# Attention and a feed-forward on one core: which tiles TensorE turns, a replanned order, and one pair's scores in float32

## The chip, the cores and the metric

The kernel runs on one core of a Trainium2 chip. The metric is the device time of one execution in microseconds (us); several executions are timed and their median is compared. PE is TensorE, PEld its weight loads, DVE VectorE, ACT ScalarE, POOL GpSimd, SP SyncE, whose queue (SPq) issues the DMAs here.

## The reference: what is computed

Two stages follow each other. The first is attention with a capped score over 4 batches, 12 heads, 448 tokens and 64 channels per head; the second is a feed-forward over all 4 x 448 = 1792 tokens.

```python
scores = scale * np.matmul(q, k.transpose(0, 1, 3, 2))
scores = cap * np.tanh(scores / cap)
attn = np.exp(scores - max); attn = attn / (sum + 1e-09)
x = np.matmul(attn, v)                       # [1792, 768] after the heads are joined
h = x @ w_in                                 # [1792, 1024]
solu = h * softmax(h)
ln = (solu - mean) / np.sqrt(var + 1e-06) * g_ln
out = ln @ w_out                             # [1792, 768]
```

(The middle lines are abridged.) Everything is float32, so a product of two float32 matrices is either one float32 matmul, which the trace shows as two instructions, or three matmuls of the float32r type: each operand is split into a high part and a low rest, and high x high, high x low and low x high are added.

## The kernel before

**Attention.** Two heads make a pair, six pairs a batch, 24 pairs in all. `front(u)` loads the pair's keys and queries (tile raw, line 362), splits them into hi and lo (lines 371 and 372), and computes the scores in three chunks of 128 keys by three float32r products (tile s, line 382) and the remaining 64 keys by one float32 product (line 387). ACT takes tanh out of PSUM (lines 392 and 410) into ea and eb and then exp in place (line 395). `back(u)` multiplies the exponentials by the values in float32 (tile pv, lines 463 and 468), and sums them over the keys by small matmuls into tile z (line 477). From pair 8 on DVE adds chunks first (lines 442 to 448), which halves that work. `divide(b)` turns a batch's sums into reciprocals (lines 527 to 536) and multiplies xt, the transposed attention output, by them.

**Feed-forward.** The 1792 tokens are 14 tiles of 128; tiles 0 to 2 need batch 0 alone, 3 to 6 also batch 1, 7 to 9 batch 2, 10 to 13 batch 3. `ff_in(t)` splits the tile into xh and xl (lines 558 and 559) and runs 36 matmuls of 512 columns (lines 568 to 570) into the two PSUM buffers of the ring m, then `keep`, exp, the sums and the normalisation on DVE, ACT and POOL (lines 575 to 615). `ff_out(t)` runs 48 matmuls of 384 columns (lines 678 to 680), through the same ring m. Between them the normalised tile has to be turned, so that its channels lie on partitions. There are two ways, and one condition chooses, at lines 617 and 640:

```python
if BY_DVE <= t < NTILE - BY_PE:
```

If it holds, DVE transposes 32 x 32 blocks (line 620), SP issues 16 DMAs that gather the blocks (line 625), a copy makes the high part (line 649) and DVE the low part (line 650). If not, PE turns the tile by eight transposes against an identity, four into each of two PSUM buffers (line 664), a copy out of PSUM makes the high part (line 667), and DVE the low part (line 668). The buffers come from m, or from the scores' ring s for tiles 9 and later. Before the change BY_DVE is 1 and BY_PE 1, so tiles 1 to 12 go by DVE and the DMAs, and tiles 0 and 13 by PE.

**Weights.** w_in and w_out arrive as 64-bit words; ACT and DVE convert each of 12 and 16 chunks (lines 721 to 732) while the first pairs run.

**The order.** Nothing is scheduled by hand. Every piece of work is a `step` with an engine, a cost, a due time and its reads and writes; `Plan.run` simulates the engines, always lets the engine that can start first take the ready step with the earliest due time, and then writes each engine's instructions in that order. Engines execute strictly in that order, so an instruction that has to wait holds everything behind it on its engine. The due times come from the constants at the head of the file (UNIT, AHEAD1, WI_FROM, ...), and the waits between engines from LATENCY, TO_PE and FROM_PE. Copies that ACT or DVE can do go to the one that the planner thinks will end first.

Of the kernel before, what the change touches and what calls it, by code (L numbers as in the profile page):

```python
# [9 lines left out]
F32 = mybir.dt.float32  # L10
# [1 line left out]
I32 = mybir.dt.int32  # L12
CAP_MAX = 40.0
HOLD = 0.1
LATENCY = 0.15
T0 = 4.0
UNIT0 = 0.71
UNIT = 6.29
TILE = 13.13
CUTS0 = (128, 256, 384)  # L20
CUTS1 = (64, 192, 320)
CUTS2 = (128, 256, 384)
CUTS3 = (64, 192, 320)
LATER = 17.82
EARLY = -9.62
LEAD0 = 0.16
LEAD1 = 0.41
LEAD2 = 5.35
LEAD3 = 1.36
AHEAD1 = 21.64  # L30
AHEAD2 = 57.26
AHEAD3 = 79.39
WI_FROM = -0.47
WI_STEP = 2.15
WO_FROM = 1.45
WO_STEP = 4.91
ADDS_FROM = 8
CH1 = -1.8
CH2 = -39.84
REST_AT = -1.96  # L40
EXPA = 0.63
EXPB = -0.6
SUMA = 0.62
SUMB = 4.88
VAL = 4.2
VALSTEP = 0.45
ZAT = 2.64
RAWS = 2
LOS = 1
VS = 2  # L50
WARM = 5
BY_PE = 1
BY_DVE = 1
TURN_AHEAD = 6.88
GATHER = 5.4
HS = 2
# [4 lines left out]
MM448 = 0.2035  # L61
MM384 = 0.1743
TURN = 0.128
SWITCH = 0.1
STAY = 41.15
BIAS = 0.21
TO_PE = 0.25
FROM_PE = 0.2
HEAD1 = 0.11
AF = mybir.ActivationFunctionType  # L70
ALU = mybir.AluOpType
# [72 lines left out]
def PRODUCTS(hi, lo):  # L144

    return (hi, hi), (hi, lo), (lo, hi)
# [34 lines left out]
class Plan:  # L181
# [6 lines left out]
    COPY = "ACT or DVE"  # L188

    def __init__(self, nc, free):  # L190
        self.steps, self.free, self.tiling = [], dict(free), None
        self.copy = {"ACT": nc.scalar.copy, "DVE": nc.vector.tensor_copy}

    def step(self, eng, us, due, emit, reads=(), writes=(), lag=0.0, uses=(), tiling="128x128"):

        n = dict(eng=eng, us=us, tiling=tiling, due=due, emit=emit, lag=lag, deps=[], starts=[], todo=0, outs=[], start=None, i=len(self.steps))
        for t in reads:
            n["deps"] += t.writers
        for t in writes:
            if t.first is None:  # L200
                t.first = n
                if t.prev is not None:
                    n["deps"] += t.prev.writers + t.prev.readers
# [16 lines left out]
    def run(self):  # L220
        for n in self.steps:
            n["todo"] = len(n["deps"]) + len(n["starts"])
            for d in n["deps"] + n["starts"]:
                d["outs"].append(n)
        ready = {eng: [] for eng in ("PE", "ACT", "DVE", "POOL", "SP", self.COPY)}
        for n in self.steps:
            n["at"] = 0.0
            if not n["todo"]:
                ready[n["eng"]].append(n)
        order = []  # L230
        while any(ready.values()):
            best = None
            for eng, free in self.free.items():
                other = {"ACT": "DVE", "DVE": "ACT"}.get(eng)
                ns = ready[eng]
                if other:
                    ns = ns + [n for n in ready[self.COPY] if self.end(n, eng) <= self.end(n, other)]
                if not ns:
                    continue
                first = max(free, min(n["at"] for n in ns))  # L240
                n = min((n for n in ns if n["at"] <= first), key=lambda n: (n["due"], n["i"]))
                us = n["us"] if n["eng"] == eng else n["us"][eng]
                n = min((n for n in ns if n["at"] <= first + self.HOLD * us), key=lambda n: (n["due"], n["i"]))
# [12 lines left out]
            if eng == "PE" and n["tiling"] != self.tiling:  # L256
                n["us"] += SWITCH
                self.tiling = n["tiling"]
            n["start"] = start
            self.free[n["eng"]] = start + n["us"]  # L260
            order.append(n)
            for m in n["outs"]:
                m["todo"] -= 1
                wait = self.WAIT.get((n["eng"], m["eng"]), LATENCY) + n["us"] + n["lag"]
                m["at"] = max(m["at"], start + (wait if any(d is n for d in m["deps"]) else 0.0))
                if not m["todo"]:
                    ready[m["eng"]].append(m)
# [12 lines left out]


def dve(n, rate=1, extra=0):
    return n / rate / 960 + 0.068 + 0.061 * extra
# [3 lines left out]
def body(ctx: ExitStack, tc, kq, v, w_in, w_out, g_ln, out, r_tanh, r_exp, mhalf, sel, sels, ident, gT, xtail, both, guard, general, const=None, loaded=None):  # L287

    nc = tc.nc
    B, NP, P, S = kq.shape  # L290
    D, S = P // 2, S // 2
    NC = S // P
    REST = S - NC * P
# [18 lines left out]
    hi_r, lo_r = ring("hi", 2, [P, 2 * S - REST], F32R), ring("lo", LOS, [P, 2 * S - REST], F32R)  # L312
# [19 lines left out]
    step = plan.step  # L332
# [15 lines left out]
    def front(u):  # L348
# [12 lines left out]
        p.place = [half[j if u % 2 == 0 else 1 - j] for j in range(2)]  # L361
        step("SP", 1.6, due - (1.5 * d if u else 20.0), lambda: nc.sync.dma_start(out=raw.get(), in_=kq[b, p.hp]), writes=[raw], lag=2.0)

        hi, lo = hi_r.new(), lo_r.new()
        at = due - 0.5 * d
        n = 2 * S - REST

        for x in ((slice(0, n),) if u else (slice(0, n - S), slice(n - S, n))):
            part = Buf()
            m, r = x.stop - x.start, slice(REST + x.start, REST + x.stop)  # L370
            step(plan.COPY, copied(m), at, lambda copy, x=x, r=r: copy(out=hi.get()[:, x], in_=raw.get()[:, r]), [raw], [hi, part])  # L371
            step("DVE", dve(m), at, lambda x=x, r=r: nc.vector.tensor_sub(lo.get()[:, x], raw.get()[:, r], hi.get()[:, x].bitcast(F32)), [raw, part], [lo])

        ea, eb = p.ea, p.eb = ea_r.new(), eb_r.new()
        p.chunk = lambda c: ea.get()[:, 2 * c:2 * c + 2] if c < 2 else eb.get()[:, :2]
        p.rest = lambda j: eb.get()[p.place[j], 2]

        def scores(c, pt):
            parts = [(x.get(), y.get()) for x, y in PRODUCTS(hi, lo)]
            for i, (x, y) in enumerate(parts):  # L380
                for j in range(2):
                    nc.tensor.matmul(pt.get()[:, j, :S], lhsT=x[half[j], c * P:(c + 1) * P], rhs=y[half[j], NC * P:], start=(i == 0), stop=(i == len(parts) - 1))  # L382
# [5 lines left out]

        def chunk(c, at):
            pt = s_r.new()  # L390
            step("PE", len(PRODUCTS(0, 0)) * MM448, at, lambda: scores(c, pt), [hi, lo], [pt], tiling="64x128")
            step("ACT", act(2 * S, 0.05), at, lambda: nc.scalar.activation(out=p.chunk(c), in_=pt.get()[:, :, :S], func=AF.Tanh, scale=r_tanh), [pt], [ea if c < 2 else eb])  # L392

        def exp(e, k, at):
            step("ACT", act(k * S), at, lambda: nc.scalar.activation(out=e.get(), in_=e.get(), func=AF.Exp, scale=r_exp), [e], [e])  # L395
# [1 line left out]
        def rest(at):  # L397
            pt = s_r.new()

            def both_rests():  # L400
                scores_rest(pt)
                if old:
                    old.values_rest()

            if old:
                step("PE", 4 * MM448, at, both_rests, [raw, old.v, old.eb], [pt, old.pp], tiling="64x64")["starts"] += old.pp.writers[:-1]
                old.finish()
            else:
                step("PE", 4 * MM448, at, both_rests, [raw], [pt], tiling="64x64")
            step("ACT", act(S, 0.05), at, lambda: nc.scalar.activation(out=eb.get()[:, 2], in_=pt.get()[:, 0, :S], func=AF.Tanh, scale=r_tanh), [pt], [eb])  # L410

        def load_v():
            step("SP", 0.8, due - (d if u else 19.0), lambda: nc.sync.dma_start(out=p.v.get(), in_=v[b, p.hp]), writes=[p.v], lag=2.0)
# [336 lines left out]
    if not general:  # L750

        idle = pv_r.new()

        def warm():
            x = xtail.rearrange("p k d -> p (k d)")
            for i in range(WARM):
                nc.tensor.matmul(idle.get()[:, :2 * P], lhsT=x[:, :P], rhs=x[:, P:], start=True, stop=True)

        step("PE", 0.7 * WARM, -100.0, warm, writes=[idle])
    front(0)  # L760
    for b in range(B):
        for hp in range(NP):
# [56 lines left out]
```

## Time and profile before

| | |
|---|---|
| median of the runs, lowest, highest | 431.03, 430.65, 434.64 us |
| the profiled execution | 435.72 us |
| its span, from first to last instruction | 433.9 us |
| busy, share of the span | PE 95%, PEld 65%, DVE 70%, ACT 55%, POOL 11% |
| mean granted TensorE clock over the span | 0.986 |
| chain that ended last, by engine | PE 56%, DVE 13%, ACT 8%, SPq 8%, DMA 8% |

The chain follows the work back from the last instruction, at each step to what released it. A busy PE is not PE at its peak: matmuls are pipelined, their ends are modelled, and one matmul's record overlaps the next one's. What a piece of PE work costs is therefore read from the start of one group of instructions to the start of the next.

### The profile page before, as it was taken

The page shows a single profiled execution, that of the slowest core. Times are in us where ns is not written, and L with a number is a line of the kernel's source. Part 1 is how long each engine was busy: PE and PEld are TensorE (multiplying, and loading weights), DVE is VectorE, ACT ScalarE, POOL GpSimd, SP SyncE. Part 2 cuts the span into 40 slices and gives each one's busy share as a digit, 9 for nine tenths or more (in the row PEclk, how much of TensorE's full clock was granted, in tenths as well). Part 3 has the DMA queues.
Part 4 walks back from the last instruction along what each step waited for, and adds up shares of the span by engine and source line. Part 5 has one row for each costly group of instructions (what it writes and reads, how often), then busy time and mean ns, then how long its engine had stood idle before and what let it go on. Part 6 is the DMA issues. An engine that isn't in the chain of part 4 may idle for free.

```text
span 433.9 us, 6550 instructions
## 1 busy us (share of the span) xinstructions
PE 410.5 (95%) x2314; PEld 282.3 (65%) x2314; DVE 302.7 (70%) x736; ACT 239.3 (55%) x317; POOL 46.6 (11%) x122
## 2 busy tenths in 40 slices
PE   7789799999997999999999989999999999999894
PEld 4333334667742348888964445666877898998894
DVE  3889979999986899665538499977543984643310
ACT  4889799478776984261339988195321320221220
POOL 2000000022400000112212000011110111211100
PEclk9699899999999999999999999999999999999999
DMA  7778965000234330121223432102011111111111
GB/s 249 282 246 295 315 212 180 2 0 6 59 107 156 128 104 24 44 61 37 71 69 120 130 113 84 63 23 64 23 50 37 51 51 41 63 48 50 57 59 42
DMA packets 25418, 41.43 MB, mean 95 GB/s; under 512 B 5920, under 2 KB 18720, under 8 KB 25376
## 3 DMA queue, kind: packets, MB, share of 16 engines
q1 hardware_dynamic: 25376, 40.92, 29.1%
q8 instruction: 20, 0.33, 0.3%
q14 instruction: 22, 0.18, 0.1%
HBM read 29.10 MB, written 5.51 MB: 80 GB/s over the span
## 4 chain that ended last, share of the span: by engine, by line
PE 56%; DVE 13%; ACT 8%; SPq 8%; DMA 8%; issue 3%; POOL 2%; DVEq 0%; ACTq 0%; POOLq 0%
PE pv L463 8%; PE s L382 7%; SPq L625 7%; PE m L678 7%; PE m L680 6%; PE m L679 6%; PE m L568 6%; PE m L569 6%; PE m L570 5%; DMA wi<-in_w_in 3%; PE s L387 3%; DMA raw<-in_kq 2%; ACT ea L392 2%; PE z L477 2%; DVE rs L535 2%
## 5 line engine op out<-in xcount | busy, mean ns | idle before, releaser
L678 PE MATMUL m<-wo,ln 128*128 128x384 f32 x208 | 71.0, 342 | 0.3 <-DVE h L575 0.3
L679 PE MATMUL m<-wo,ln 128*128 128x384 f32 x208 | 69.8, 336 | 0.4 <-DVE wo L732 0.4
L680 PE MATMUL m<-wo,ln 128*128 128x384 f32 x208 | 69.7, 335 | 0.0
L568 PE MATMUL m<-wi,xh 128*128 128x512 f32 x168 | 66.6, 397 | 0.5 <-DVE ln L668 0.5
L570 PE MATMUL m<-wi,xl 128*128 128x512 f32 x168 | 65.9, 392 | 0.1
L569 PE MATMUL m<-wi,xh 128*128 128x512 f32 x168 | 65.8, 392 | 0.0
L463 PE MATMUL pv<-ea,v 128*64 128x448 f32 x192 | 46.0, 589 | 8.4 <-ACT eb L410 3.3
L392 ACT ACTIVATE ea<-s 128x896 f32<-128x896 f32 x48 | 41.5, 918 | 15.7 <-PE s L382 15.7
L586 ACT ACTIVATE ef<-h,st 128x1024 f32<-128x1024 f32 x14 | 16.1, 1153 | 56.7 <-DVE h L575 33.9
L678 PEld LDWEIGHTS m<-wo,ln 128*128 128x128 f32 x208 | 39.0, 188 | 3.7 <-issue 2.6
L395 ACT ACTIVATE ea<-ea 128x1792 f32<-128x1792 f32 x24 | 40.9, 1702 | 0.5
L679 PEld LDWEIGHTS m<-wo,ln 128*128 128x128 f32 x208 | 39.1, 188 | 2.0 <-DVE wo L732 0.8
L568 PEld LDWEIGHTS m<-wi,xh 128*128 128x128 f32 x168 | 31.5, 188 | 11.6 <-issue 3.8
L680 PEld LDWEIGHTS m<-wo,ln 128*128 128x128 f32 x208 | 39.0, 188 | 0.0
L382 PEld LDWEIGHTS s<-hi 64*128 64x128 f32 x144 | 13.8, 188 | 35.4 <-issue 14.9
L591 POOL TENSOR_SCALAR st<-st 128x1 f32<-128x1 f32 x14 | 8.6, 616 | 260.8 <-ACT ef L586 260.7
L570 PEld LDWEIGHTS m<-wi,xl 128*128 128x128 f32 x168 | 31.5, 188 | 7.3 <-DVE xl L559 0.5
L569 PEld LDWEIGHTS m<-wi,xh 128*128 128x128 f32 x168 | 31.5, 188 | 5.7
L382 PE MATMUL s<-hi 64*128 64x448 f32 x144 | 32.0, 441 | 3.3 <-DVE hi L371 1.6
L395 ACT ACTIVATE eb<-eb 128x1344 f32<-128x1344 f32 x24 | 32.0, 1333 | 0.3
L463 PEld LDWEIGHTS pv<-ea,v 128*64 128x64 f32 x192 | 12.0, 142 | 30.2 <-issue 14.8
L687 ACT COPY o<-m 128x384 f32<-128x384 f32 x24 | 11.5, 478 | 34.7 <-PE m L680 32.1
(120 smaller groups left out, 742.0 us busy)
## 6 DMA issues: line engine op xcount, KB each, us to landing
raw<-in_kq SPq DMA_DIRECT2D x24, 448.0 KB, 3.9
ef<-h SPq DMA_DIRECT2D x192, 32.0 KB, 1.8
wo<-in_w_out SPq DMA_DIRECT2D x15, 384.0 KB, 6.8
wi<-in_w_in SPq DMA_DIRECT2D x11, 512.0 KB, 8.0
v<-in_v SPq DMA_DIRECT2D x24, 224.0 KB, 2.7
out<-o SPq DMA_DIRECT2D x28, 192.0 KB, 1.9
ln<-in_w_in SPq DMA_DIRECT2D x1, 512.0 KB, 7.1
es<-in_w_out SPq DMA_DIRECT2D x1, 384.0 KB, 7.9
```

What stands on the lines that cost most here:

```text
L382: nc.tensor.matmul(pt.get()[:, j, :S], lhsT=x[half[j], c * P:(c + 1) * P], rhs=y[half[j], NC * P:], start=(i == 0), stop=(i == len(parts) ...
L392: step("ACT", act(2 * S, 0.05), at, lambda: nc.scalar.activation(out=p.chunk(c), in_=pt.get()[:, :, :S], func=AF.Tanh, scale=r_tanh), [pt] ...
L395: step("ACT", act(k * S), at, lambda: nc.scalar.activation(out=e.get(), in_=e.get(), func=AF.Exp, scale=r_exp), [e], [e])
L463: nc.tensor.matmul(t[half[j], :S], lhsT=vv[:, j * NC + c], rhs=p.chunk(c)[:, j], start=(c == 0), stop=False, skip_group_check=True)
L568: nc.tensor.matmul(pt.get(), lhsT=a, rhs=w[:, 0], start=(kk == 0), stop=False)
L569: nc.tensor.matmul(pt.get(), lhsT=a, rhs=w[:, 1], start=False, stop=False)
L570: nc.tensor.matmul(pt.get(), lhsT=l, rhs=w[:, 0], start=False, stop=(kk == KD - 1))
L586: step("ACT", act(DFF, 0.093, 2), at, lambda: nc.scalar.activation(out=e.get(), in_=hh.get(), func=AF.Exp, bias=m()[:, 1:2], scale=-1.0, a ...
L625: nc.sync.dma_start(out=e.get()[q * 32:q * 32 + 32, i * n:i * n + n], in_=hh.get()[i * 32:i * 32 + 32, q * n:q * n + n])
L678: nc.tensor.matmul(p, lhsT=a, rhs=w[:, 0], start=(f == 0), stop=False)
L679: nc.tensor.matmul(p, lhsT=a, rhs=w[:, 1], start=False, stop=False)
L680: nc.tensor.matmul(p, lhsT=l, rhs=w[:, 0], start=False, stop=(f == KF - 1))
```

## The change

Three things change. BY_DVE goes from 1 to 7, so that tiles 1 to 6 are turned by PE as tile 0 is. The first pair (`F32_UNTIL = 1`) is not split: its three chunks of scores are float32 matmuls on raw, and its casts and subtractions are gone. And the planner gets other waits (LATENCY, TO_PE, FROM_PE), other due times, and a dearer tanh (0.11 instead of 0.05 in `act`), which reorders all engines. A filler of idle PE time is added but is off (`FILL = False`). Names such as raw, ea and m are the same; lines lie 8 to 24 further down.

```diff
-LATENCY = 0.15
+LATENCY = 0.22
-UNIT0 = 0.71
-UNIT = 6.29
-TILE = 13.13
+UNIT0 = 0.26
+UNIT = 5.54
+TILE = 11.99
...
+F32_UNTIL = 1
+FILL = False
...
-BY_DVE = 1
+BY_DVE = 7
...
-TO_PE = 0.25
-FROM_PE = 0.2
+TO_PE = 0.27
+FROM_PE = 0.4
...
-        hi, lo = hi_r.new(), lo_r.new()
+        plain = u < F32_UNTIL
+        hi, lo = (None, None) if plain else (hi_r.new(), lo_r.new())
...
         def scores(c, pt):
+            if plain:
+                x = raw.get()
+                for j in range(2):
+                    nc.tensor.matmul(pt.get()[:, j, :S], lhsT=x[half[j], REST + c * P:REST + (c + 1) * P], rhs=x[half[j], S:], start=True, stop=True)
+                return
...
-            step("PE", len(PRODUCTS(0, 0)) * MM448, at, lambda: scores(c, pt), [hi, lo], [pt], tiling="64x128")
+            step("PE", (4 if plain else len(PRODUCTS(0, 0))) * MM448, at, lambda: scores(c, pt), [raw] if plain else [hi, lo], [pt], tiling="64x128")
```

Three places show how the order moves. The first is ACT at the start of the kernel, in the kernel before; o is the scratch of the weight conversion, wi_121 the first chunk of w_in.

```order
L127 ACTIVATE guard<-ecap 128x1
L133 TENSOR_LOAD tscale
L410 ACTIVATE eb<-s 128x448
L722 ACTIVATE o<-wi_121 128x512
L392 ACTIVATE ea<-s 128x896 x2
L722 ACTIVATE o<-wi_129 128x512
L727 CAST wi_171<-o 128x512
L133 TENSOR_LOAD ecap
L395 ACTIVATE ea<-ea 128x1792
```

And the same place after the change.

```order
L130 ACTIVATE guard<-ecap 128x1
L136 TENSOR_LOAD tscale
L421 ACTIVATE eb<-s 128x448
L403 ACTIVATE ea<-s 128x896
L733 ACTIVATE o<-wi_121 128x512
L403 ACTIVATE ea<-s 128x896
L733 ACTIVATE o<-wi_126 128x512
L136 TENSOR_LOAD ecap
L406 ACTIVATE ea<-ea 128x1792
L403 ACTIVATE eb<-s 128x896
```

One of the two tanh of the first pair (ea<-s) now stands ahead of the first weight copy (o<-wi_121), and a cast of w_in has left ACT.

The second place is SP's queue from the first gather on, during batch 1, in the kernel before; ef<-h x16 is the gather of one tile.

```order
L625 DMA ef<-h 32x256 x16
L688 DMA out<-o 128x384
L413 DMA v<-in_v 128x448
L362 DMA raw<-in_kq 128x896
L625 DMA ef<-h 32x256 x16
L413 DMA v<-in_v 128x448
L362 DMA raw<-in_kq 128x896
L688 DMA out<-o 128x384
L362 DMA raw<-in_kq 128x896
L413 DMA v<-in_v 128x448 x2
L362 DMA raw<-in_kq 128x896
```

And after the change, from the same load on.

```order
L424 DMA v<-in_v 128x448
L370 DMA raw<-in_kq 128x896
L699 DMA out<-o 128x384
L424 DMA v<-in_v 128x448
L370 DMA raw<-in_kq 128x896
L699 DMA out<-o 128x384
L370 DMA raw<-in_kq 128x896
L424 DMA v<-in_v 128x448 x2
L370 DMA raw<-in_kq 128x896
L424 DMA v<-in_v 128x448
L370 DMA raw<-in_kq 128x896
```

The two gathers are gone from between the loads of v and raw; stores of out still stand between them.

The third place is PE at the end of `ff_out(1)` (m<-wo,ln), in the kernel before: `ff_in(4)` (m<-wi) follows directly.

```order
L678 MATMUL m<-wo_1266,ln 128x384
L679 MATMUL m<-wo_1266,ln 128x384
L680 MATMUL m<-wo_1266,ln 128x384
L568 MATMUL m<-wi_171,xh 128x512
L569 MATMUL m<-wi_171,xh 128x512
L570 MATMUL m<-wi_171,xl 128x512
```

After the change the first four transposes of tile 2 (m<-ident,ef) follow, and then a pair of attention.

```order
L690 MATMUL m<-wo_1242,ln 128x384
L691 MATMUL m<-wo_1242,ln 128x384
L675 MATMUL m<-ident,ef 128x128 x4
L488 MATMUL z<-es,sel 32x448 x4
L393 MATMUL s<-hi 128x448 x2
L393 MATMUL s<-lo,hi 128x448 x2
L393 MATMUL s<-hi,lo 128x448 x2
L393 MATMUL s<-hi 128x448 x2
L393 MATMUL s<-lo,hi 128x448 x2
L393 MATMUL s<-hi,lo 128x448 x2
L474 MATMUL pv<-ea,v 64x448 x4
```

The other four transposes of tile 2 stand at the end of that pair, ahead of `ff_in(4)`.

```order
L479 MATMUL pv<-eb,v 64x448 x2
L393 MATMUL s<-hi 128x448 x2
L393 MATMUL s<-lo,hi 128x448 x2
L393 MATMUL s<-hi,lo 128x448 x2
L675 MATMUL m<-ident,ef 128x128 x4
L579 MATMUL m<-wi_157,xh 128x512
```

Of the twelve new groups of four transposes most stand like these, one behind matmuls of `ff_out`, one at the end of a pair.

## Rows read from the trace of the kernel before

**Rows 1.** Windows by stage: start:end, length, busy PE PEld DVE ACT POOL, PEclk, DMA share, GB/s.

```profile
0.00:73.26 73.26, 63.17 (x396) 26.62 (x396) 58.09 (x124) 62.20 (x81) 2.69 (x22) 0.93 0.74 254
73.26:160.93 87.67, 83.34 (x482) 47.75 (x481) 80.18 (x205) 67.32 (x90) 10.75 (x22) 1.00 0.23 73
160.93:345.00 184.07, 182.76 (x1018) 133.72 (x1017) 127.25 (x317) 92.60 (x119) 22.48 (x50) 1.00 0.21 65
```

**Rows 2.** Waits, PE in 0 to 73 us: us in total, times, longest.

```profile
PE pv L463 <- ACT eb L410: 3.3, 2, 2.3
PE pv L463 <- ACT ea L395: 2.6, 1, 2.6
```

**Rows 3.** Waits, ACT in 7.3 to 72 us.

```profile
ACT ea L392 <- PE s L382: 2.7, 3, 1.4
ACT o L722 <- DMA wi<-in_w_in: 1.7, 2, 0.9
ACT o L722 <- DMA ln<-in_w_in: 0.9, 1, 0.9
```

**Rows 4.** Timeline of ACT: start us, us, engine line op, out<-in, count, idle before and releaser.

```profile
8.21 0.66 ACT L722 ACTIVATE o<-wi 128x512 f32<-128x512 f32 x1 [0.89 <-DMA wi<-in_w_in]
...
71.77 0.84 ACT L558 CAST xh<-xt 128x768 fp32r<-128x768 f32 x1
```

**Rows 5.** Timeline of PE: the same eight matmuls twice.

```profile
49.97 3.26 PE L463 MATMUL pv<-ea,v 128*64 128x448 f32 x8 [2.28 <-ACT eb L410]
...
59.01 1.72 PE L463 MATMUL pv<-ea,v 128*64 128x448 f32 x8
```

**Rows 6.** Timeline of SP's queue, gathers (ef<-h) and loads (raw).

```profile
121.04 10.02 SPq L625 DMA_DIRECT2D ef<-h  x16
...
131.73 0.43 SPq L362 DMA_DIRECT2D raw<-in_kq  x1
...
234.33 10.23 SPq L625 DMA_DIRECT2D ef<-h  x16
```

**Rows 7.** Timeline of PE: where a pair of batch 1 begins.

```profile
131.56 1.59 PE L477 MATMUL z<-es,sel 128*32 128x448 f32 x8
```

**Rows 8.** Chain that ended last, 120 to 152 us: start us, us, what.

```profile
131.73 4.01 DMA raw<-in_kq
...
142.04 0.97 PE pv L463 x4
...
144.42 1.66 PE pv L463 x8
...
149.59 1.42 PE s L382 x12
151.00 0.95 PE z L527 x2
```

**Rows 9.** Waits, PE from 73 us to the end.

```profile
PE s L382 <- DVE hi L371: 1.6, 2, 0.8
PE s L382 <- DVE lo L372: 1.1, 2, 0.6
PE pv L463 <- DMA v<-in_v: 0.8, 1, 0.8
PE m L678 <- DVE xt L649: 0.7, 1, 0.7
```

**Rows 10.** Timeline of PE: second half of tile 0's transposes, and what follows.

```profile
94.62 0.66 PE L664 MATMUL m<-ident,ef 128*128 128x128 f32 x4
95.79 0.50 PE L568 MATMUL m<-wi,xh 128*128 128x512 f32 x1 [0.51 <-DVE ln L668]
```

**Rows 11.** Timeline of PE: tile 13's transposes, and what follows.

```profile
415.27 1.03 PE L664 MATMUL s<-ident,ef 128*128 128x128 f32 x8
416.06 0.42 PE L678 MATMUL m<-wo,xt 128*128 128x384 f32 x1
```

**Rows 12.** Chain that ended last: one pair's products with the values.

```profile
229.40 2.41 PE pv L463 x12
```

More of the change, by code (lines that the diff above doesn't have):

```diff
@@ L23 @@
 CUTS3 = (64, 192, 320)
[L24 to L36, printed above, removed]
-ADDS_FROM = 8
[L38 to L47, printed above, removed]
+LATER = 7.03
+EARLY = -7.09
+LEAD0 = -0.17
+LEAD1 = 0.64
+LEAD2 = 3.18
+LEAD3 = -0.44
+AHEAD1 = 1.73
+AHEAD2 = 59.83
+AHEAD3 = 74.11
+WI_FROM = -0.0
+WI_STEP = 1.99
+WO_FROM = 7.28
+WO_STEP = 3.44
+ADDS_FROM = 8
+CH1 = -4.86
+CH2 = -21.54
+REST_AT = -0.18
+EXPA = 0.48
+EXPB = -0.67
+SUMA = 0.19
+SUMB = 26.44
+VAL = 3.4
+VALSTEP = 1.25
+ZAT = 1.7
 RAWS = 2
@@ L51 @@
 WARM = 5
+F32_UNTIL = 1
+FILL = False
+FILL_FROM = 0.5
 BY_PE = 1
-BY_DVE = 1
+BY_DVE = 7
 TURN_AHEAD = 6.88
@@ L64 @@
 SWITCH = 0.1
-STAY = 41.15
+STAY = 47.68
 BIAS = 0.21
-TO_PE = 0.25
-FROM_PE = 0.2
+TO_PE = 0.27
+FROM_PE = 0.4
 HEAD1 = 0.11
@@ L190, in __init__ @@
     def __init__(self, nc, free):
-        self.steps, self.free, self.tiling = [], dict(free), None
+        self.steps, self.free, self.tiling, self.fill = [], dict(free), None, None
         self.copy = {"ACT": nc.scalar.copy, "DVE": nc.vector.tensor_copy}
@@ L268, in run @@
         assert len(order) == len(self.steps)
+        end = None
         for n in order:
+            if n["eng"] == "PE":
+                if self.fill and end is not None:
+                    self.fill(n["start"] - end)
+                end = n["start"] + n["us"]
             n["emit"]()
@@ L362, in front @@
         step("SP", 1.6, due - (1.5 * d if u else 20.0), lambda: nc.sync.dma_start(out=raw.get(), in_=kq[b, p.hp]), writes=[raw], lag=2.0)
-        hi, lo = hi_r.new(), lo_r.new()
+        plain = u < F32_UNTIL
+        hi, lo = (None, None) if plain else (hi_r.new(), lo_r.new())
         at = due - 0.5 * d
         n = 2 * S - REST
[L368 to L372, printed above, removed]
+        if not plain:
+            step(plan.COPY, copied(n), at, lambda copy: copy(out=hi.get(), in_=raw.get()[:, REST:]), [raw], [hi])
+            step("DVE", dve(n), at, lambda: nc.vector.tensor_sub(lo.get(), raw.get()[:, REST:], hi.get().bitcast(F32)), [raw, hi], [lo])
         ea, eb = p.ea, p.eb = ea_r.new(), eb_r.new()
@@ L390, in chunk @@
             pt = s_r.new()
-            step("PE", len(PRODUCTS(0, 0)) * MM448, at, lambda: scores(c, pt), [hi, lo], [pt], tiling="64x128")
-            step("ACT", act(2 * S, 0.05), at, lambda: nc.scalar.activation(out=p.chunk(c), in_=pt.get()[:, :, :S], func=AF.Tanh, scale=r_tanh), [pt], [ea if c < 2 else eb])
+            step("PE", (4 if plain else len(PRODUCTS(0, 0))) * MM448, at, lambda: scores(c, pt), [raw] if plain else [hi, lo], [pt], tiling="64x128")
+            step("ACT", act(2 * S, 0.11), at, lambda: nc.scalar.activation(out=p.chunk(c), in_=pt.get()[:, :, :S], func=AF.Tanh, scale=r_tanh), [pt], [ea if c < 2 else eb])
         def exp(e, k, at):
@@ L409, in rest @@
                 step("PE", 4 * MM448, at, both_rests, [raw], [pt], tiling="64x64")
-            step("ACT", act(S, 0.05), at, lambda: nc.scalar.activation(out=eb.get()[:, 2], in_=pt.get()[:, 0, :S], func=AF.Tanh, scale=r_tanh), [pt], [eb])
+            step("ACT", act(S, 0.11), at, lambda: nc.scalar.activation(out=eb.get()[:, 2], in_=pt.get()[:, 0, :S], func=AF.Tanh, scale=r_tanh), [pt], [eb])
         def load_v():
@@ L752, in body @@
         idle = pv_r.new()
+        if FILL:
+            bank = z_r.make()
+            z_r.make = lambda: bank
         def warm():
             x = xtail.rearrange("p k d -> p (k d)")
+            if FILL:
+                nc.tensor.matmul(bank[:, S:], lhsT=x[:, :P], rhs=x[:, :D], start=True, stop=True)
             for i in range(WARM):
@@ L759, in body, with fill @@
         step("PE", 0.7 * WARM, -100.0, warm, writes=[idle])
+        if FILL:
+            def fill(gap):
+                for i in range(min(40, int((gap - FILL_FROM) / 0.12))):
+                    nc.tensor.matmul(bank[:, S:], lhsT=ident, rhs=ident[:, :D], start=False, stop=True, skip_group_check=True)
+            plan.fill = fill
     front(0)
```

## The prediction

> **What bounds the kernel now.** I read the busy time by stage first, because a share over the whole span hides where PE stands still. Three stages matter. Until 73.26 us, where the first `ff_in` starts, PE is busy 63.17 of 73.26 us, while ACT has 62.20 and DVE 58.09 [rows 1]: the weights are converted there beside the first pairs, and PE waits. From 73.26 to 160.93 us (batch 1's attention with the first feed-forward tiles) PE lacks 87.67 - 83.34 = 4.3 us, from there to 345 us 184.07 - 182.76 = 1.3 us [rows 1]. After that it runs almost without a gap until its last tile. So the kernel is PE's, apart from the first stage, and two kinds of edit count: what adds work to PE costs its full length after 73 us, and what removes a wait gives it back.
>
> Second I read who ends PE's waits. In the first stage it is ACT, 3.3 and 2.6 us in the longest two groups [rows 2]. ACT in turn, from its first tanh on, stands still mainly in three groups, 2.7 + 1.7 + 0.9 = 5.3 us [rows 3]: it waits for scores of PE, and twice an instruction of the weight conversion, placed ahead of a tanh or an exp, waits for its DMA and holds them, as at 8.21 us for 0.89 us [rows 4]. A third loss hangs on it: after PE stood still for 2.28 us, its next eight matmuls took 3.26 us where the same eight take 1.72 at 59.01 us [rows 5]. The granted clock of the stage is 0.93 for that reason, 1.00 in the next two [rows 1].
>
> After 73 us the waits are for loads. A gather keeps SP's queue for 10 us: the one at 121.04 us ends at 131.06, and the load of a pair's raw stands behind it, issued at 131.73 [rows 6]. It lands 4.01 us later [rows 8]. From 131.56 [rows 7] to 142.04 us PE does the work of one pair in 10.48 us; the same steps without a wait take 144.42 to 151.00 us, 6.58 us [rows 8]. That is 3.9 us lost. The gather at 234.33 us does it once more to a later pair: the waits for hi and lo have two cases each, 1.6 and 1.1 us in all [rows 9], so the second is worth half, about 1.4 us.
>
> **The change part by part.**
>
> *The gathers of tiles 1 to 6 go.* With them go 6 x 16 DMAs and the two delays, 3.9 + 1.4 = -5.3 us. What is late next is the raw load itself, behind stores of out, which wait for a copy out of PSUM. The order has one such store between loads where it had gathers, and a store waits less than the 10 us of a gather; but it can be all of it, so the bounds are -5.3 and 0. I take -5.3, since after the change nothing between the loads takes longer than one issue once its data is there.
>
> *Six tiles are turned on PE.* That is 6 x 8 = 48 transposes in twelve groups of four. Tile 13's eight, dense, take from 415.27 to 416.06 us, 0.79 [rows 11]: 0.40 for four, 12 x 0.40 = 4.7 us. The second four of tile 0 took 0.66 us to their end, followed by a wait of 0.51 for the low part to leave PSUM [rows 10]: 12 x 0.66 = 7.9 us without that wait. Between the ends I take 0.45 a group, +5.4 us, near the dense row, because most groups stand with work before and behind them that needs nothing of them. This is work on the path, after 73 us, and nothing hides it. What DVE loses (six transposes, and the longer copies) and what ACT gains (copies out of PSUM) lies beside PE, whose idle time in these stages is not theirs except for 1.5 us.
>
> The Trainium skill speaks against this part. The row shows eight transposes in 0.79 us, one per 0.11 us though each record is longer, at a granted clock of 1.00 in a stage that holds tile 0's two groups [rows 1, 11]. The page "TensorE: Matmul & The Clock Gate", section "Part 4: PE-mode transpose", gives about 275 ns for a 128 x 128 transpose inside a kernel, and says that transposes do not count as activity for the clock. By its price the 48 would be 13.2 us, an estimate, and the sum 7.8 us higher; I go by the row. What its second statement would do is a rival below.
>
> *The first pair in float32.* PE does 12 float32 instructions for 18 float32r ones. Twelve of the first kind take 2.41 us [rows 12], eighteen of the second 18/12 x 1.42 = 2.13 [rows 8]: +0.3 us of PE. It is hidden, since PE waits for ACT there; and PE need not wait for a cast and two subtractions of DVE. If that cover is gone it costs 0.3. Bounds +0.3 and -0.9 (ACT's first wait at 8.21); its gain is counted in the next part.
>
> *The order of the first stage.* ACT's list up to the first xh at 71.77 us [rows 4] is nearly as long as before: five casts of w_in go to DVE and four copies of xt come from it, of similar size. So only waits can go. The first tanh of ea no longer stands behind the weight copy that waits for a DMA, and the copy of the last w_in chunk now stands behind an exp. The waits for scores follow partly from PE's slow matmuls. I take a little under half of the 5.3 us, -2.4. At worst nothing comes back, because the loads keep the DMAs busy for 0.74 of the stage [rows 1]; at best all of it, -5.3.
>
> *Longer planned waits in the rest.* Idle time after 73 us is 4.3 + 1.3 = 5.6 us; the groups for hi, lo and v that hang on the raw delay hold 1.6 + 1.1 + 0.8 of it [rows 9], so about 2 us remain. I take -0.5, bounds 0 and -2. The end stays: tiles 7 to 12 keep their gathers, and PE's wait for tile 12's high part, 0.7 us [rows 9], with it.
>
> Sum: -5.3 + 5.4 - 2.4 - 0.5 = -2.8 us. The profiled execution took 435.72 us, a span of 433.9 and 1.8 around it, and would take 432.9. It is 4.7 us above the median of the runs, 431.03, so the same 2.8 taken off the median give **428.2 us**, 0.7% faster. One per cent, about what a measurement of this kernel can tell from no change, is 4.3 us.
>
> **The rivals.**
>
> *The first stage opens up.* If no instruction of ACT waits for a DMA ahead of a tanh, PE's 2.28 us pause and the slow matmuls after it go as well. Then the stage gives 5.3, the later waits 2.0, and the transposes cost the dense price 4.7: -5.3 - 5.3 - 2.0 + 4.7 = -7.9, or 423.1 us. For it: the same wait starts both losses [rows 2, 3, 5]. Against it: ACT and DVE have 62 and 58 us of work in 73 [rows 1].
>
> *The transposes wait for PSUM, slower than before.* Each half needs a buffer of the ring m, which `ff_in` and `ff_out` also need. If each group stands still as tile 0's second did, it costs 0.66 + 0.51 = 1.17 us [rows 10], 14.0 in all, and the sum is -5.3 - 2.4 - 0.5 + 14.0 = +5.8, or 436.8 us. It passes +1% from 1.04 us a group. For it: the only such row shows it. Against it: the new groups have a pair of attention or an `ff_in` between them, not one z block.
>
> *The raw loads are late anyhow,* behind the stores of out. Then 5.3 stays: +2.5 us, 433.5. For it: the stores stand in the same place of the queue. Against it: no gather among them.
>
> *The clock falls.* If transposes let the granted clock drop to its lower level of 1.2 GHz, each of the twelve groups could be followed by a stretch like that at 49.97 us, 3.26 - 1.72 = 1.5 us lost [rows 5]: 12 x 1.5 = 18 us, 446. That is the rule of the same page of the Trainium skill. Against it is the clock of 1.00 around tile 0's groups [rows 1].
>
> **How the numbers follow.** Chances: my forecast 0.48, with a range of its own of 426 to 431 us; the opened first stage 0.28; late loads 0.12; the wait for PSUM 0.10; the clock 0.02. The low end of the range lies at the opened stage, 423, with a little for the clock's share at the start, 422.5; the high end reaches past the late loads to part of the PSUM case, 434.5. Faster by over 1% (under 426.7) are the second case and a fifth of mine, 0.38; slower by over 1% (over 435.3) the last two, 0.12; between them 0.50.
>
> **What would show it.** Right: the first `ff_in` starts near 71 us; no wait for hi or lo by a raw load between 73 and 270 us; twelve more groups of transposes of 0.4 to 0.5 us from start to next start, with the clock at 1.00 around them; the wait for tile 12 still there. Wrong: waits of a transpose or of the `ff_in` behind it for a copy out of PSUM, a raw issued behind a waiting store, or an `ff_in` that starts before 69 us, with a first-stage clock well over 0.93.

## The result, and the profile after

| | before | after |
|---|---|---|
| median, and range, of the compared runs | 434.04 us (430.65 to 435.02, 11 runs) | 428.6 us (426.76 to 430.77, 11 runs) |
| profiled execution, span | 435.72, 433.9 us | 429.13, 427.3 us |
| first `ff_in` starts | 73.26 us | 66.76 us |
| from there to the last 66 matmuls of `ff_out` ahead of tile 13's transposes | 328.8 us | 326.0 us |
| those 66 matmuls | 13.22 us | 15.81 us |

The ratio is 0.9882, with a 95% interval of 0.9855 to 0.9908: 1.2% faster. The time of 428.6 us lies next to the forecast of 428.2, but the difference does not: the forecast took 2.8 us off 431.03, the median of the three runs shown ahead of the prediction, and 5.4 went from 434.04, the median of the eleven compared here. The spans of the two profiled executions differ by 6.5 us: 6.5 went in the first stage and 2.8 in the middle; 2.6 came back in the last 66 matmuls and 0.2 behind them.

The windows by stage answer to [rows 1]. Columns as there.

```profile
0.00:66.76 66.76, 60.99 (x391) 25.05 (x391) 54.56 (x121) 60.62 (x80) 2.69 (x22) 0.97 0.80 279
...
149.96:332.24 182.28, 182.28 (x1040) 134.93 (x1039) 116.68 (x300) 95.53 (x126) 19.41 (x50) 1.00 0.16 52
...
392.75:408.56 15.81, 13.55 (x68) 12.90 (x67) 5.22 (x10) 3.44 (x6) 1.98 (x7) 0.89 0.14 44
```

Compare the length with PE's busy time. The first stage lost 6.5 us of length, 4.3 of them idle time of PE and 2.2 busy time, its clock rose from 0.93 to 0.97, and 182 us in the middle have no idle time at all. New is the third line, the last 66 matmuls ahead of tile 13's transposes: a granted clock of 0.89, where the same matmuls of the kernel before had 1.00.

```profile
402.06:415.27 13.21, 11.95 (x67) 11.31 (x66) 4.95 (x9) 3.88 (x7) 1.98 (x7) 1.00 0.19 61
```

The waits of PE from the first `ff_in` to the end answer to [rows 9].

```profile
PE m L691 <- DVE st L610: 1.6, 1, 1.6
PE m L689 <- DVE xt L660: 0.7, 1, 0.7
PE s L393 <- DVE lo L378: 0.3, 1, 0.3
PE pv L474 <- ACT ea L406: 0.3, 1, 0.3
```

The waits for hi (1.6) and v (0.8) are gone, and that for lo fell from 1.1 us to 0.3. With them went the raw load behind a gather. A wait of 1.6 us in the end is new. The waits of ACT in the first stage, from 7.3 to 66 us, answer to [rows 3].

```profile
ACT eb L421 <- PE s L398: 2.1, 1, 2.1
ACT ea L403 <- PE s L388: 0.4, 1, 0.4
ACT ea L403 <- PE s L393: 0.3, 1, 0.3
```

Both waits for a weight's DMA have gone, and what is left are 2.8 us for scores. The transposes, in the timeline of PE, answer to [rows 10, 11]; columns: start us, us, instruction.

```profile
109.82 0.60 PE L675 MATMUL m<-ident,ef 128*128 128x128 f32 x4
110.36 0.47 PE L393 MATMUL s<-hi 64*128 64x448 f32 x2
...
197.53 0.66 PE L675 MATMUL m<-ident,ef 128*128 128x128 f32 x4
197.94 0.48 PE L579 MATMUL m<-wi,xh 128*128 128x512 f32 x1
...
408.56 1.03 PE L675 MATMUL s<-ident,ef 128*128 128x128 f32 x8
409.35 0.42 PE L689 MATMUL m<-wo,xt 128*128 128x384 f32 x1
```

From start to next start a group costs 0.53 us in the first of these rows, ahead of a pair's scores, and 0.41 in the second, ahead of `ff_in`; the longest take 0.59. The twelve new groups sum to 5.85 us, 0.49 each, with no wait in front of any.

The chain that ended last, by engine, on the page: before the change SPq and DMA had 8% each.

```profile
PE 69%; ACT 12%; DVE 10%; issue 2%; SPq 2%; POOL 2%; DMA 0%; ACTq 0%; DVEq 0%; POOLq 0%
```

The queue and the transfers are off it, PE has 69% of it instead of 56%. Now the end, PE first. L689 and L690 use tile 12's high part, L691 its low part.

```profile
399.82 0.41 PE L689 MATMUL m<-wo,xt 128*128 128x384 f32 x1 [0.66 <-DVE xt L660]
400.07 0.34 PE L690 MATMUL m<-wo,xt 128*128 128x384 f32 x1
402.01 0.60 PE L691 MATMUL m<-wo,xt 128*128 128x384 f32 x1 [1.60 <-DVE st L610]
402.40 0.53 PE L689 MATMUL m<-wo,xt 128*128 128x384 f32 x1
...
405.75 0.34 PE L691 MATMUL m<-wo,xt 128*128 128x384 f32 x1
```

And DVE beside it, in the same stretch.

```profile
398.98 0.69 DVE L660 CAST xt<-ef 128x1024 fp32r<-128x1024 f32 x1 [5.28 <-DMA ef<-h]
399.59 1.22 DVE L607 SCALAR_TENSOR_TENSOR ef<-h,ef 128x1024 f32<-128x1024 f32 x1
400.74 0.08 DVE L607 DVE_READ_ACCUMULATOR ef<-h,ef 128x1 f32 x1
400.74 1.22 DVE L661 TENSOR_TENSOR xt<-ef,xt 128x1024 fp32r<-128x1024 f32 x1
```

DVE makes tile 12's high part, then a product of tile 13 (L607), then tile 12's low part (L661), to 401.96 us. The profile writes L610 as the releaser at 402.01, the instruction that follows L661; what PE needed is L661. Before the change the low part stood ahead of that product, and PE waited 0.58 us for it:

```profile
406.95 1.23 DVE L650 TENSOR_TENSOR xt<-ef,xt 128x1024 fp32r<-128x1024 f32 x1
408.09 1.22 DVE L596 SCALAR_TENSOR_TENSOR ef<-h,ef 128x1024 f32<-128x1024 f32 x1
...
408.23 0.44 PE L680 MATMUL m<-wo,xt 128*128 128x384 f32 x1 [0.58 <-DVE xt L650]
```

After the pause of 1.60 us a matmul's record takes 0.53 us where it takes 0.33 to 0.34, for 3.4 us in which the granted clock is 0.50: its lower level.

### The profile page after: what moved, and what is told of

Same layout as the page of the kernel before. It is cut to its first block, busy times and chain, and to the rows that moved or that the text cites. A ratio compares the mean times of both kernels' runs of the same rounds, so it can differ in the third digit from the quotient of the medians.

```text
span 427.3 us, 6497 instructions
## 1 busy us (share of the span) xinstructions
PE 412.3 (96%) x2356; PEld 287.8 (67%) x2356; DVE 291.3 (68%) x729; ACT 243.5 (57%) x326; POOL 44.1 (10%) x122
## 4 chain that ended last, share of the span: by engine, by line
PE 69%; ACT 12%; DVE 10%; issue 2%; SPq 2%; POOL 2%; DMA 0%; ACTq 0%; DVEq 0%; POOLq 0%
PE pv L474 9%; PE m L689 8%; PE m L691 8%; PE m L690 8%; PE s L393 7%; PE m L579 7%; PE m L580 7%; PE m L581 7%; PE s L398 3%; ACT ea L403 3%; SPq L636 2%; PE z L488 2%; ACT ea L406 2%; ACT eb L406 2%; ACT o L733 1%
## 5 line engine op out<-in xcount | busy, mean ns | idle before, releaser
L689 PE MATMUL m<-wo,ln 128*128 128x384 f32 x208 | 70.6, 340 | 0.0
L691 PE MATMUL m<-wo,ln 128*128 128x384 f32 x208 | 69.7, 335 | 0.0
L690 PE MATMUL m<-wo,ln 128*128 128x384 f32 x208 | 69.7, 335 | 0.0
L474 PE MATMUL pv<-ea,v 128*64 128x448 f32 x192 | 42.8, 564 | 4.2 <-ACT ea L406 2.8
L602 POOL TENSOR_SCALAR st<-st 128x1 f32<-128x1 f32 x14 | 9.7, 692 | 307.7 <-ACT ef L597 307.7
L689 PEld LDWEIGHTS m<-wo,ln 128*128 128x128 f32 x208 | 39.0, 188 | 3.0 <-issue 1.7
L690 PEld LDWEIGHTS m<-wo,ln 128*128 128x128 f32 x208 | 39.1, 188 | 1.1 <-issue 0.2
L691 PEld LDWEIGHTS m<-wo,ln 128*128 128x128 f32 x208 | 39.0, 188 | 0.0
L626 DVE TENSOR_SCALAR ef<-ef,st 128x1024 f32<-128x1024 f32 x14 | 11.4, 812 | 32.9 <-POOL st L623 32.9
L393 PE MATMUL s<-hi 64*128 64x448 f32 x138 | 30.5, 438 | 0.0
```

What stands on the lines that cost most here:

```text
L474: nc.tensor.matmul(t[half[j], :S], lhsT=vv[:, j * NC + c], rhs=p.chunk(c)[:, j], start=(c == 0), stop=False, skip_group_check=True)
L689: nc.tensor.matmul(p, lhsT=a, rhs=w[:, 0], start=(f == 0), stop=False)
L690: nc.tensor.matmul(p, lhsT=a, rhs=w[:, 1], start=False, stop=False)
L691: nc.tensor.matmul(p, lhsT=l, rhs=w[:, 0], start=False, stop=(f == KF - 1))
```

## The experiments

What each kernel did to the three stretches, from its profiled execution, and its time:

| kernel | first `ff_in` | to the last 66 | those 66 | median | ratio to before, interval |
|---|---|---|---|---|---|
| by7only | 70.40 | 329.8 | 13.23 | 433.93 | 1.002, 0.998 to 1.006 |
| f32only | 75.93 | 333.6 | 13.23 | 438.23 | 1.011, 1.004 to 1.017 |
| planonly | 67.55 | 345.1 | 13.80 | 447.19 | 1.030, 1.023 to 1.038 |
| before_gq | 69.11 | 323.5 | 11.45 | 425.15 | 0.982, 0.976 to 0.988 |
| before_again | 71.94 | 332.1 | 13.21 | 437.63 | one run |
| after_pe12 | 66.30 | 338.3 with the 66 | | 425.71 | 0.981, 0.976 to 0.985 |
| after_gq | 67.17 | 326.2 | 12.47 | 425.83 | 0.982, 0.977 to 0.987 |
| by1_gq | 66.50 | 326.9 | 11.80 | 426.54 | 0.984, 0.978 to 0.991 |
| after_swap | 67.74 | 326.1 | 14.00 | 428.40 | 0.985, 0.981 to 0.990 |
| by5_gq | 66.48 | 324.5 | 11.82 | 424.20 | 0.976, 0.972 to 0.981 |
| by4_gq | 68.50 | 323.9 | 16.31 | 427.58 | 0.983, 0.976 to 0.990 |
| by3_gq | 67.78 | 323.4 | 11.82 | 424.02 | 0.975, 0.971 to 0.979 |

**One part alone: the turning on PE (by7only).** The kernel before, with

```diff
-BY_DVE = 1
+BY_DVE = 7
```

> The kernel before with BY_DVE = 7 alone. Theory (gathers held the loads of raw, transposes cost 0.4 to 0.6 us a group): the first ff_in starts at 73.3 us as before; the waits of PE for hi and lo behind a raw load go, -5.3 us; twelve groups of transposes cost 5.9 us; sum +0.6 us, ratio 0.995 to 1.005. Rival (the gain of the whole change after 73 us comes from this part too, other waits of PE going with the gathers): -2.8 us, ratio 0.990 to 0.995. Rival (loads of raw stay late behind the stores of out): +5.9 us, ratio 1.013.

It is as fast as before. The middle is 329.8 us, 1.1 longer than before: 6.0 us of transposes come, from start to next start in its own trace, and 5.3 of raw delays go, +0.7 by the sum. The waits for hi and lo behind a raw load are gone from its list. The trade alone is worth nothing measurable; the change's gain comes from elsewhere.

**One part alone: the first pair in float32 (f32only).** The changed code with the old constants, old waits and BY_DVE = 1, but

```diff
+F32_UNTIL = 1
```

> The kernel before with the first pair's scores in float32 and nothing else; the planner's constants are the old ones. Theory (the first stage became shorter through the order of ACT's work, not through this pair): the first ff_in starts at 71.5 to 73.3 us, ratio 0.995 to 1.000. Rival (the first pair's cast and subtractions were what delayed the whole stage): the first ff_in starts at 67 to 68 us, -6 us, ratio 0.985 to 0.988.

Slower by 1%, which neither theory had forecast. In the profiled execution, 443.26 us and so 5 us over the median, the first `ff_in` starts at 75.93 us, later than in any other kernel, since the planner's answer to the shorter first pair puts z's matmuls behind an exp that ends late (PE waits 4.2 us for it at 13.9 us). Since the planner reorders around it, this run doesn't price the pair alone. It shows that the pair doesn't bring the first stage's gain by itself.

**One part alone: the plan (planonly).** The changed constants and waits, with the first pair split as before and DVE turning tiles 1 to 12:

```diff
-F32_UNTIL = 1
+F32_UNTIL = 0
-BY_DVE = 7
+BY_DVE = 1
```

> The kernel after with BY_DVE = 1 and the first pair split as before: the planner's new waits, costs and due times alone. Theory (order of ACT's work in the first stage): the first ff_in starts at 67 to 69.5 us; the gathers and the late loads of raw stay, 5 us of waits; ratio 0.985 to 0.992. Rival (the first pair makes the gain): the first ff_in starts at 72 to 73.5 us, ratio 0.997 to 1.003.

It has the early first `ff_in`, 67.55 us, so that gain is the plan's: of the eight executions with the first pair in float32 and the same plan, shown below, the earliest has 66.30 us and the latest 68.50. But the middle takes 345.1 us, 16.3 more than before, and the kernel is 3% slower. PE's waits in the middle sum to 16.6 us instead of about 6, and the granted clock was at its lower level for 13.7 us of it, where the profile before has none. The timelines of SP's queue, DVE and PE show the costliest case.

```profile
207.12 10.01 SPq L638 DMA_DIRECT2D ef<-h  x16
217.23 0.53 SPq L370 DMA_DIRECT2D raw<-in_kq  x1
...
220.69 0.59 DVE L379 CAST hi<-raw 128x832 fp32r<-128x832 f32 x1 [6.97 <-DMA raw<-in_kq]
221.20 0.68 DVE L588 TENSOR_SCALAR_CACHE_REDUCE h<-m 128x512 f32<-128x512 f32 x1
...
221.95 0.44 PE L691 MATMUL m<-wo,ln 128*128 128x384 f32 x1 [4.78 <-DVE h L588]
```

One gather holds the queue for 10.01 us; the raw load behind it leaves at 217.23; DVE stands 6.97 us before the cast of that raw, because its order puts the cast first; `keep` (L588), which would free a PSUM buffer, stands behind the cast; and PE waits 4.78 us for the buffer. A gather cost 3.9 us at most before; here it is dearer. The parts of the change don't add: the plan needs the gathers out of that queue. (by1_gq, below, has this plan, the float32 pair and all twelve gathers, but in another queue; its middle is 18.2 us shorter.)

**The gathers in another queue (before_gq).** The kernel before, every gather issued by GpSimd:

```diff
-                        nc.sync.dma_start(out=e.get()...
+                        nc.gpsimd.dma_start(out=e.get()...
```

> The kernel before with the 16 DMAs of each gather issued from GpSimd's queue and not from SP's; every other instruction stands where it stood. Theory (the loads of raw are late because SP's queue is held for 10 us): no load of raw is issued behind a gather, the waits of PE for hi and lo at 136 and 250 us go, the stretch from 73 to 345 us is shorter by 4 to 5.3 us. Rival (the loads are late because the buffer of raw is freed late, or the DMAs are busy with the gather): the waits at 136 and 250 us stay and the stretch keeps its 271.7 us within 1.

The middle falls to 323.5 us, by 5.3: the size that the prediction gave to the two raw delays, with not one transpose more on PE. This one-word edit of the kernel before gains 1.8%, where the whole change gains 1.2% (the two intervals overlap). The waits of PE from 72 us on begin so:

```profile
PE m L568 <- DVE ln L668: 0.5, 1, 0.5
PE pv L463 <- ACT ea L395: 0.3, 1, 0.3
```

Nothing waits for hi, lo or tile 12 any more. The last 66 matmuls take 11.45 us instead of 13.22, because a gather holds its queue for less time there. In after_gq the one of tile 12 reads, in the timeline of POOL,

```profile
387.88 7.92 POOL L636 DMA_DIRECT2D ef<-h  x16 [3.78 <-DVE h L631]
```

which is 7.92 us, 0.50 a DMA, where SP took 10.02 [rows 6]. The Trainium skill, page "DMA: Bandwidth & Descriptors", section "Issuing engine by pattern", holds that DMAs issued by SP are generally faster than GpSimd's. These rows don't bear that out for 16 small copies from SBUF to SBUF, and what counted more was what else stands in the queue.

**The kernel before once more (before_again).** No edit.

> The kernel before, unchanged, for a second profile. Theory (the first stage varies from run to run by some us, through when the weights land and whether the clock falls after the pause near 50 us): the first ff_in starts somewhere from 69 to 73.5 us, everything after it as in the first profile within 0.5 us. Rival (the first stage is the same each time): 73.3 us.

Its first `ff_in` starts at 71.94 us; with by7only and before_gq, which have the same order up to there, the old plan gives 73.26, 71.94, 70.40 and 69.11, mean 71.2. The new order gives 66.76, 66.30, 67.17, 66.50, 67.74, 66.48, 68.50 and 67.78 in the changed kernel and its variants, mean 67.2. So the new order gains 4.0 us in the first stage in the mean; 6.5 was a difference between two single executions. The theory is missed behind it: the middle, 332.1, is 3.3 us over that of the other execution of the same kernel, where 0.5 was allowed. The windows show why.

```profile
136.00:137.10 1.10, 0.71 (x6) 0.68 (x8) 1.10 (x2) 0.00 (x0) 0.00 (x0) 1.00 0.19 67
137.10:140.50 3.40, 3.40 (x18) 0.90 (x14) 2.98 (x5) 3.33 (x3) 0.00 (x0) 0.51 0.01 2
```

After the waits for hi and lo of the late raw load (1.00 and 0.56 us) the granted clock is 0.51 for 3.4 us; after the second late load at 253.2 us it falls again. In the first execution the same waits (0.85 and 0.57 us) left it at 1.00. The raw delays therefore cost more in some executions than the 5.3 us that before_gq saves against the first.

**The last tiles' turning (after_pe12).** The changed kernel, with tile 12 turned by PE too:

```diff
-BY_PE = 1
+BY_PE = 2
```

> The kernel after with tile 12 too turned by PE (BY_PE = 2). Theory (PE waits for tile 12's gather and for its low part, which stands behind tile 13's product on DVE, and then runs slowly because it stood still): the 4.4 us above the dense rate in the last 66 matmuls of w_out ahead of tile 13's transposes go, eight transposes cost 0.8 us, -3.5 us against the kernel after; ratio to before 0.980. Rival (tile 13's own chain sets the end anyhow): PE waits ahead of tile 13's transposes instead, within 1 us of the kernel after, ratio 0.987.

From the first `ff_in` to tile 13's transposes it takes 338.3 us, the changed kernel 341.8: 3.5 us less, although eight more transposes run. The waits of PE from 72 us on are these two alone.

```profile
PE s L393 <- DVE lo L378: 0.3, 1, 0.3
PE pv L474 <- ACT ea L406: 0.3, 1, 0.3
```

**The changed kernel with its six gathers on GpSimd (after_gq).** The edit of before_gq.

> The kernel after with the gathers of tiles 7 to 12 issued from GpSimd's queue, all else in place. Theory (after the change no load stands behind a gather any more; the only gather that PE still waits for is tile 12's): nothing changes from the first ff_in to the last ff_out of tile 11, the end is 2 to 3.5 us shorter; ratio to before 0.979 to 0.983. Rival (gathers on SP still cost in the middle): the middle gets shorter by over 1.5 us as well.

The middle is as long as in the changed kernel, 326.2 against 326.0: its remaining gathers stood in nobody's way there. The end falls to 12.47 us, and the median is 2.8 us below the changed kernel's, nearly as much as with tile 12 on PE (2.9).

**The order of two instructions (after_swap).** The changed kernel; only L607 of tile 13 goes behind L661 of tile 12 on DVE.

> Only one thing differs from the changed kernel: at the end DVE subtracts tile 12's low part directly behind its high part, and does tile 13's product after it; every other instruction of every engine stands where it was. Theory A (the end grew by 2.6 us because the low part stood 1.22 us behind the product, so that PE waited 1.60 us for it at 402 us and then ran at half the clock for 3.4 us): the low part is there 1.2 us earlier, the wait of 1.60 us at the low part falls to under 0.5, the clock stays at 1.00 there, and the last 66 matmuls ahead of tile 13's transposes take 13.0 to 14.0 us instead of 15.81; in the time -1.5 to -2.6 us against the changed kernel (428.6), about 426.5. Tile 13's transposes start up to 1.2 us later against their product only if the chain product, mean, variance, normalisation now ends behind the 66 matmuls. Theory B (the end grew because PE reaches it earlier and tile 13's own chain sets it): the 66 matmuls take less but a wait of about the same size stands ahead of tile 13's transposes, time unchanged (428.6 within 0.5).

PE's timeline:

```profile
401.98 0.44 PE L691 MATMUL m<-wo,xt 128*128 128x384 f32 x1 [0.58 <-DVE xt L661]
402.26 0.33 PE L689 MATMUL m<-wo,xt 128*128 128x384 f32 x1
...
407.80 1.09 PE L675 MATMUL s<-ident,ef 128*128 128x128 f32 x8 [0.66 <-DVE ef L626]
```

The wait for the low part fell from 1.60 to 0.58 us, just over the bound of 0.5 that was set, and the matmuls behind it take 0.33 us: no fall of the clock. But a wait of 0.66 us stands now ahead of tile 13's transposes, since tile 13's normalisation is the later for it. The stretch took 14.00 us instead of 15.81. Theory A had 13.0 to 14.0 for it. The median, 428.40, is only 0.2 us below the changed kernel's, where Theory A had about 426.5. In the profiled execution 1.0 of the 1.8 us went in a later first `ff_in`, at 67.74, in a stage whose clock stood at its lower level for 6.8 us instead of 3.4. Beside the kernel before, the ratio is 0.985 against the changed kernel's 0.988, and the intervals overlap. The mechanism is shown by the rows, its gain in the time is not.

**Fewer tiles on PE, gathers on GpSimd (by1_gq, by5_gq, by4_gq, by3_gq).** after_gq with one constant:

```diff
-BY_DVE = 7
+BY_DVE = 1
```

and 5, 4 and 3 in the others.

> The kernel after with BY_DVE = 1 again, so that tiles 1 to 12 are turned by DVE and gathers, and the gathers on GpSimd's queue. Theory (the only use of turning tiles 1 to 6 on PE was to free SP's queue; its price is 5.9 us of PE): 5.9 us less than after_gq, ratio to before 0.965 to 0.970. Rival (the new order itself does not bear the gathers, as the planner's part alone was slower by 3%): the waits of planonly stay, ratio 1.00 or more.

The transposes go, and the middle is not shorter (326.9). Neither forecast came true: the ratio is 0.984, above the theory's 0.965 to 0.970 and below the rival's 1.00. DVE and PE at 118 to 121 us:

```profile
118.78 1.01 DVE L378 TENSOR_TENSOR lo<-raw,hi 128x832 fp32r<-128x832 f32 x1
119.71 0.61 DVE L743 SCALAR_TENSOR_TENSOR wo<-o,gT,wo 128x384 fp32r<-128x384 f32 x1
...
120.37 0.69 PE L690 MATMUL m<-wo,ln 128*128 128x384 f32 x1 [2.25 <-DVE wo L743]
120.86 0.52 PE L691 MATMUL m<-wo,ln 128*128 128x384 f32 x1
```

The turning of tile 1 on DVE (from 116.65 us) pushes the last chunk of w_out behind it, and `ff_out(0)` waits 2.25 us for that. The windows give the rest of the loss:

```profile
120.40:127.20 6.80, 6.05 (x26) 2.91 (x26) 5.69 (x8) 5.60 (x6) 6.32 (x13) 0.50 0.31 92
```

For 6.8 us the clock stands at half. The other three kernels leave that place alone. Their expectations were written in the order by3_gq, by4_gq, by5_gq, so that "the last one" is each time the kernel with one tile more on DVE.

> As the last one, with tiles 5 to 12 on DVE: four groups fewer than with tiles 7 to 12, -2.0 us in the middle. Theory A: middle 324.2 us, time about 424, and 0.98 us slower than with tiles 4 to 12. Theory B: 425 to 427, with new waits of PE for DVE.

> As the last one, with tiles 4 to 12 on DVE: six groups of transposes fewer than with tiles 7 to 12, -2.9 us in the middle. Theory A: middle 323.3 us, time about 423. Theory B: new waits of PE for DVE, 424.5 to 427. If A holds for both, this one is 1.0 us slower than the one with tiles 3 to 12.

> The changed kernel with tiles 3 to 12 turned by DVE and all gathers on GpSimd's queue; the order up to tile 3's turning is that of the changed kernel. Compared with the same kernel with only tiles 7 to 12 on DVE and GpSimd (425.8 us, from the first ff_in to the last 66 matmuls 326.2 us) eight groups of transposes go, 8 x 0.49 = 3.9 us. Theory A (the turning on PE costs its measured length and a gather that is not in SP's queue costs nothing): the middle is 322.2 us and the time about 422, 2.6% faster than the kernel before. Theory B (in this plan DVE is on the path of the middle too, as with tiles 1 to 12 on DVE, where a copy for w_out waited behind it for 2.3 us): new waits of PE for DVE take back half or more, time 424 to 427.

Against after_gq the middle is shorter by 1.6, 2.3 and 2.8 us for 4, 6 and 8 groups fewer, 0.35 to 0.41 a group: less than the 0.49 that a group takes, but most of it. The time of by5_gq, 424.20, is Theory A's; by3_gq lies 2 us above Theory A's time and at the edge of Theory B's, but without B's new waits: none of PE is over 0.33 us after 67 us. It has the lowest median of all, 424.02 us, 2.5% below before, though by5_gq can't be told from it. by4_gq misses both theories: its middle gains, but its end takes 16.3 us. In the profiled execution the last gather is the reason: PE waits 1.16 and 1.60 us for tile 12's two parts, and the granted clock falls to its lower level for 3.4 us behind them.

```profile
389.89 7.92 POOL L636 DMA_DIRECT2D ef<-h  x16 [6.71 <-issue]
```

Tile 12's blocks were turned by 386.66 us, and the gather started 3.2 us later, where after_gq's started 0.3 us after (386.35 + 1.24 to 387.88). The profile names nothing that it waited for, and the kernel's four times spread from 425.7 to 430.7. In by3_gq tile 11's gather starts as late once (372.00 us, its blocks turned by 368.78), and no wait of PE comes of it. What held the two stays open.

## Why the prediction was right and where it was wrong

*The gathers' raw delays, -5.3.* Right, and shown twice: moving the gathers out of the queue alone took 5.3 us off the middle (before_gq), and the waits for hi behind a raw load disappeared whenever the gathers left that queue. "Nothing between the loads takes longer than one issue" was wrong in detail: in the changed kernel two loads of v hold SP's queue for 6.62 us from 123.72, and stores of out, said to wait less than a gather's 10 us, wait there for up to 15.3. But no wait of PE for hi comes of either. The rival of late loads falls.

*The transposes, +5.4.* Right: 5.85 us for the twelve groups, 0.49 each against 0.45. Those ahead of an `ff_in` cost 0.41, near the dense 0.40, the others up to 0.59. No group waited for PSUM, so that rival falls. Tile 0's own two groups became cheaper besides, 2.1 to 1.1 us, since the new order puts other work where it had to wait. The granted clock is 1.00 from 66.76 to 345 us with all 48 in it, so the rival of the clock falls too. The Trainium skill's price of about 275 ns each (page "TensorE: Matmul & The Clock Gate", section "Part 4: PE-mode transpose"; its example is in bfloat16) is the length of one record here too, 0.27 us, and would have made 13.2 us, an estimate. The 5.85 us measured show that a record's length is not the cost when the next matmul starts before it ends.

*The first pair, 0.* Not more than that: f32only shows no gain, and planonly, the new plan without it, has its first `ff_in` at 67.55 us, among the 66.30 to 68.50 of those with it. A cost of 0.3 us can't be seen in that spread.

*The order of the first stage, -2.4.* The right place, and the term too small: about -4.0 over the executions, -6.5 in the two profiles that the sum compares. I priced the waits of ACT alone, "a little under half of the 5.3 us", and left to a rival that PE's pauses cost more than their length. ACT's waits fell further than that, from 7.2 us, of which the three groups of the 5.3 were the largest, to 2.8. On PE itself, the windows from 0 us to the first `ff_in` show an idle time of 9.1 us in the mean of the four executions of the old order and of 6.3 in the eight of the new: 2.9 of the 4.0 us, near my term. The other 1.1 is busy time, and the granted clock goes with it, at its lower level for 6.0 and 3.8 us in the mean. The profile before was the extreme, with 10.2 us (12.4 to 19.2 and 50.0 to 53.4), where the changed kernel had 3.4 (13.0 to 16.4). At 3.4 us the old order too starts its first `ff_in` at 70.40 and 69.11 us (by7only, before_gq), 2.7 us later in the mean than the new at the same 3.4. I had also put the clock of 0.93 down to the pause ahead of 49.97 us; two thirds of that lower clock stood at 12.4 to 19.2 us, from the wait for ea [rows 2] on. The sign I named, an `ff_in` before 69 us and a clock well over 0.93, is what came: 66.76 and 0.97.

*Longer planned waits, -0.5.* Mis-sized: the middle fell by 2.8 us, of which 5.85 - 5.3 = +0.55 is explained above, so -3.3 is the plan's. 1.0 of it is tile 0's turning; the other 2.3 us spread over `ff_in`, `ff_out`, z and the values, with under 1.3 us in any of them. I can't name a single cause. About half of it can be read as waits: against by7only, which has the same transposes under the old plan and no raw delay, the middle is 3.9 us shorter, and PE's waits in it fall from 2.5 to 0.6 us, the idle time that I had put at about 2 and taken for 0.5. What planonly suggests is that these waits protect PE only as long as loads are not late.

*"The end stays."* This step failed. I took over the wait for tile 12's high part, which did stay (0.66 us), and did not look at what the new order puts on DVE between the high and the low part. It cost 2.6 us: 1.0 more of waiting (1.60 for the low part, where the same matmul waited 0.58 before), and 3.4 us at the lower clock, in which ten matmuls start 0.32 us apart; the 17 behind them start 0.17 us apart. after_swap, after_pe12 and after_gq take it away in three ways.

So the change in the profiles, -6.5 - 2.8 + 2.6 + 0.2 = -6.5, is an opened first stage, much as the first rival had it (less so over the executions), and a loss at the end that none of the cases held. That the forecast's number was met was luck: it came about because two terms that were too small and one loss that was missing partly cancelled, and because the median it started from was low.

## What to carry to other kernels

When a set of small DMAs delays loads, move it to another queue before moving the work to the busiest engine: one word in the kernel before gained 1.8%, where the whole change gained 1.2%. When a plan is recomputed, read the new order at the last tile, instruction by instruction, on the engine that feeds PE: there no later work hides a swap. And price a pause of PE in a row of matmuls with the slow matmuls that can follow it. Where they follow in some executions only, compare several executions of the same order before a difference is put down to the change.

## What the runs showed of the hardware that was not expected

A pause of PE can cost as much again afterwards. Behind the 1.60 us at 402 us, the 2.25 us at 120 us of by1_gq and the 1.00 and 0.56 us at 136 us of before_again the granted clock fell to its lower level, 1.2 GHz, for 3.4, 6.8 and 3.4 us; behind waits of 0.61 and 0.58 us in after_swap, and 0.85 and 0.57 in the kernel before, it stayed at 2.4 GHz. The length of the pause alone doesn't decide it: at the same place of the same order the kernel before paused for 2.28 us and fell [rows 5], by7only paused for 1.99 us and didn't, and before_again reads:

```profile
50.11 1.72 PE L463 MATMUL pv<-ea,v 128*64 128x448 f32 x8 [1.79 <-ACT eb L410]
```

The eight matmuls take 1.72 us here, not 3.26. Such a fall in some executions and not in others is one source of the spread between executions of one kernel.

Sixteen copies of 32 KB between places of SBUF left GpSimd's queue in 7.9 us in most gathers and SP's in 10.0.
